# Attention preparation in 512-column instructions, a transposed attention output, and a list scheduler in the kernel

## The chip, the cores and the metric

The kernel runs on one core of a Trainium2 chip. The metric is the device time of one execution, in microseconds (us), shown as the median of some runs. A profile is one further execution taken by the hardware profiler. Engines are named as it names them: PE (TensorE matmul), PEld (its weight load), DVE (VectorE), ACT (ScalarE), POOL (GpSimd), and SP (SyncE), which here only issues DMAs. An engine takes its instructions strictly in the order in which they were issued to it.

## The reference

Gated linear attention over 4 batches, 8 heads, 768 tokens and head size 48, followed by an MLP with a rational activation on the 3072 tokens of width 8 x 48 = 384:

```python
for t in range(S):
    state = alpha[:, :, t, :, None] * state + np.einsum('bhd,bhe->bhde', k[:, :, t], v[:, :, t])
    y[:, :, t] = np.einsum('bhd,bhde->bhe', q[:, :, t], state)
...
x = np.ascontiguousarray(attn_out.transpose(0, 2, 1, 3)).reshape(B * S, H * D)
...
h = x @ w_in
h2 = h * h
h3 = h2 * h
P = a[0] + a[1] * h + a[2] * h2 + a[3] * h3
Q = 1.0 + np.abs(b[0]) * np.abs(h) + np.abs(b[1]) * h2
g = P / (Q + 1e-06)
return (g @ w_out).astype(np.float32)
```

q, k, v and alpha are float32; `w_in` (384 x 2048) and `w_out` (2048 x 384) arrive as float64.

## The kernel before

The tokens are cut into 12 blocks of 256 (`m`), each of two chunks of 128 (`cc`). The recurrence is replaced by chunked products: in a chunk, running products of alpha scale q and k, the masked score matrix gives the part of y from within the chunk, and a state of 48 x 48 per head carries the rest. Heads go in four pairs `p`, one head on partitions 0 to 47 and one on 64 to 111.

**Preparation.** For a pair and block, `load_pair` (L278) brings alpha, k and q in, with four DMAs each, in pieces of 32 tokens, so that the 32 x 32 transposes of DVE (`turn_a`, `turn_k`, `turn_q`, L299 to L305, 256 columns) put the head's dimension on partitions. Two scans per chunk follow, `suffix` (L308) and `prefix` (L328), of 128 columns each, with `least` (L314) and `inverse` (L321) between them, and POOL multiplies the result into k and q (L335, L339). The first two blocks come in token by token (L352) and are transposed by PE (`turn_nat`, L363).

**A piece** is a pair in a chunk; there are 96. `sc_mm` transposes k (L390, 112 columns) and forms the scores of the two heads (L394), each head into a PSUM bank of its own. `sc_evac` copies both to SBUF with two ACT instructions (L402, L403), `sc_mask` applies the causal mask on POOL (L407), `decay` scales the state on POOL (L414). `attn_mm` then adds to y, tokens on partitions: one matmul with the state (L426), two with the scores as weights (L434), and two that form k'v for the next state (L442), which `kv_add` adds on DVE (L456, one instruction per head; L454 for the first chunk of a batch). The scores of the next piece use the same two banks and wait for this one's copies and `kv_add`.

**From y to x.** After four pieces, `y_evac` (L460) copies y, PE transposes it (L465, three matmuls), and ACT and DVE split the result in two float32r parts (L469, L473), which are the MLP's moving operand x. There are three pairs of x buffers.

**The MLP** runs in 96 units `u`: a block times one of eight groups of 256 columns of `w_in`. `mlp_in` is 18 matmuls of 256 columns (L502), then ACT, POOL and DVE compute the activation on 512 columns (L510 to L562), and `mlp_out` is 12 matmuls of 384 columns (L572 with `gh`, L582 with `gl`). Three PSUM banks hold the h of three units. The first two blocks go through weight groups 0 to 3 first and 4 to 7 afterwards (`PHASES = (0, 4)`). The weights are converted from float64 words at the start by ACT, DVE and POOL, one group of `w_in` and one of `w_out` at a time (L218 to L247).

**Order.** All steps are added to a `Plan`; the order in which they are issued was worked out beforehand and is stored in the file as a packed list (`ORDER`). Semaphores follow from the tiles that instructions share.

Beside the work, 18 DMAs read alpha once more and ACT finds out whether every value lies in the range for which the chunked products hold (L612, L616); a general path, not taken here, follows otherwise.

Of the kernel before, what the change touches and what calls it, by code (L numbers as in the profile page):

```python
# [3 lines left out]

# [18 lines left out]
class Plan:  # L23
    """Steps with an engine, a rough length and what they wait for (after, and tiles taken and
    freed).  run() calls them in the order of ORDER, after a check that each comes behind
    what it waits for."""

    def __init__(self, bufs, last):
        self.steps = {}
        self.bufs = bufs  # L30

    def add(self, key, eng, cost, fn, args, after=(), takes=(), frees=(), due=None, lat=0.2):
        self.steps[key] = (fn, args, after)

    def run(self):
        keys = list(self.steps)
        order = np.frombuffer(zlib.decompress(base64.b85decode("".join(ORDER))), np.uint16)
        assert sorted(order) == list(range(len(keys)))
        done = set()
        for n in order:  # L40
            key = keys[n]
            fn, args, after = self.steps[key]
            assert all(a in done or a not in self.steps for a in after)
            fn(*args)
            done.add(key)


TB, GB, FB = 2, 4, 2
LAG, LAG_END, PACE, T0, SLACK, EARLY = 3.0, 2.0, 5.0, 30.0, 1.3, 8
GU0, GSTEP = 40, 1.5  # L50
NAT = 2
NB0 = 2
XH, ND = 4, 4
PHASES = (0, 4)
WB = 3
HB, U0, HY = 1, 0, 0
SB, YB, XB = 3, 2, 3


# the order of the plan's steps (each by its place among the plan's add calls)  # L60
ORDER = [
    'c-jTQ0{|E{5CFhWKKbO6R9kJXwr$(CZDX~z+ICmlwr$(CvAd4Y5B`BgFctQ|N$3ilp%e6gzo8p+fc`KIro&?R7rM',
    'YG02lzHVFnC@!7vEMKm(i!|G_v|0!yJ6%!aYh6B^=jXoP*BDGq@-umS|kh4HW+8skt{3Cmy@G(!myp*hZi2{0U*;',
    '6&&P2;H$atb&oS8aBc_m=7&*EsTIkuo)J@WS9c2uq7(!4t=pbw#Egp0oFhVj0<gW6GVc&&=K3>J~##YLBnY{0G;p',
    '*w8O~I1^esI&>5q^78rqDu@`p3gK!9X<5}o|=O7jQ0r8*@UW0zv6aR$k5Fh&EV;F>g;|+KMBnIG6OaKFM7~X{QFc',
    '@#caC{24fZ!W!gOT_QUchs>0|{Y(UI&vfH4MQ|phZ;p2Mw?osDHvsNCev<f=C1Z;$Zy?#^7NXq(|Wpy$kNb5g3gZ',
    'V5mL{X(2I;#b|I5g17`0(!nd(4G~3pxCh4|2}Ba(aF`yC|KV@Q0GEN`1iXd`2;wU2fH!a-qJx8pI0JLQWPAW`!9!',
    'Ar0RfW1PWS>-FakV+_i#u51u@|(%)^|p5|6`F6yhCRfmm=?XM}0^9b&_Dj4YDFOuVn-fE4d^Qt<=s=|?&R%t9q{!',
    '2>-TAHr6MBHruVFb6ZiT#P0j>xcTIo{xFpgH8#<^#aTcPjoRDp}**bI8tYUMfg-N#^mCYM)6e}u>|wNGyPdF#pik',
    '%T2UO5i1nBimSYLX1~2pqtOEJqn_h(_;k!;HQj1ccC_BUuKXhqu!i%k_DUJB4ql(>FL{x=8#cKSe{}3;ATCoOW3Z',  # L70
    'hrK8bqgLVlAc<)#0~}LF>>E&_CKzT(JSOiW<Nai{gll7*E6`N1Lz_q!6$5W{fX9#iloU3&y2D+b|Br7U{)bA_BeD',
    '@hFQpj)HQC_*4cGh=?TVU;P0RP(m?EM<S%r`XFW(+p#eu7LjQOj?p_Yk4Q+VC<^Vu{7@58ia#hdC8FFSG3~)xkcO',
    'H-bdiMeP;rr#nnGSGEYeX@$}9F_GbjrMpd4iorA2-!B{I-HOi$&hAneCtA|o}21NbM!5}BwF9l}H+GZlhtBBO{(`',
    'RFi4qXLwLZr~AY0fnI)6cx$nC}yR<r~;LTV^{=|Q#QJcwV@zYq7zs~6sGLdfO3hVP*&s<Md&0}fQFQUDvOj<QWT|',
    'ASP{-*4$4WVu^3f?T+|Zsi!+#;ic=k^OeMrQtVkuOGL#cdL`mvGIYkv}L|tjDK95!D5q^YHR2RnSYIFh1ivprLH4',
    '>$%9#j+;alEb|YS2||OqZ|>P0&rKpco`-(iOah)kITj1-0lFHlx}!lsb#M*i=*!-RL^DhB`EiZew%mLG_`kxQ{L9',
    '4i*wOu?@7Od)S>?QCX@Y9$*9LMGx@__N3M{oE~Fus!Jm&lV~W~P$yB3`p`erLJStQ#8hfaEk#Z76kCb5FhI1UzBG',
    '*{>e`})=px!d9np^_>H0K+>WcR8H?^n9x}KO$14Re=mu6B&>QB$Gffz;0XaIE;twm?*CI-?JJ(`wNFVRMfq3U85J',
    ';zQoOf(iNXe<q)8T0}h!eAOlv*{&f7OQ9oji*;wU(BHkVGm89*LXAZ6m7*^nn)c)5Ag<@i+R*c?4|bNEzTD!X+FK',
    'f)wGX#iv=`^*3bc(Oyk8unnG)75uKwUVjV4}?&5M7A<ok{F<h*tK4PeNkH2xG*g*f$e)@p_h$VE8Hqr%}D-O{|yh',  # L80
    'NL5v{*`qsh!wN4``40gh!~a*h2q`&)82KrBUJ`O%z}77_Ac*=__uf%XFL`(Koz8PiPyRpb28C-cDEPBz>aqc#U?^',
    'DOxXf&@_FWe&7NzU5^nr=rcX08Tu!#6{qPYeW71?hMv*Y@RV*5sBbh+JSVSi(^(oTv=S<cdO^WV5_f2dm?~b<WN}',
    '(Z^@{q72<9ujCRBGRqWM94g;MwEJ4H5ch}1OklipGc72oU=M$HlL=oc*()5U*chDcz3(-N^zL@|*J7^^ypgl4G_=',
    '036d!|bH@bTK$3&EMh!B{qMWpwP?|QOz=u!6>sqL{QPpB9YNt3eimxlgLC=G0aDbq>`FUMw`egnOP&U7&6O6O!Jr',
    'dLuEDlMRH@zpK6tusZ*FFs*s6gZiU+-rHO53>B1(JnXPXJXJ(10YK}fDGMg&KnrJGUDPpRc=qk0zZgz{=;#w$XVy',
    'aEzPKc+rh%{!S$YJ7`Sn80-X%2|Erno6;a+!GMMu@F)o0TH1$z$TEY9^g2VdAR1CcP<XYM6W`zB(*QnImGeXl4?q',
    '^s2PkDvpYj>X@i*YMO+qjA?FanMCS(NUUm`{APu?63UvSs*brI%9#S@t*C2~se-1wsb~IDEldSd-}Era)owa2TA2',
    'nWg}NnrnwI9EXl=HMk*1+(WA24U=22*CQmJ0Xo9&{aX=l!e9pa=&tty%JW|x?&E1M3cw@ITqnm%Tp{>OAOY1Mq)&',
    '!khGO=Hv7EYSa&CgyK*H)K#<On>t<%rzO+8!^C~6Q@K$HQMYHmqaEt(9APgRc1BFj55DP7IjxNHDk=<FxGT655hQ',
    ';O}!TL&0y2bj5pcUMbX_1G3UhulS2(P3(Yz+(d1N@MQ%08EHLX$E_FqeRg=xba8oQYdDLR_B)kp>%ztKzDXw0Gyl',  # L90
    'RO#XjY4<=AO7JHkb$Eniyu5nt1Yr*ktmlWu~$kZt|;#V!1hFMwkNXm$)D{npa}8nPyg)=i!4Wq~42XVx@T`wwOC&',
    'x>=}yidCktI$~y+t!9yaCuW)(qKJ|*u3W4ynZxEkT~vJ($INB3%@k9g#8GqH%r+&|cJnN(HapA-v&NKE-@{H*UtK',
    'XEOR4MPq}gTGn$qf&d17{(GU~CoW=@;Da*ugxUWPN~iMVdcsb}V?NGI=$v*w#AudW&)&lxQ%s8>PB&*FypZX(Ev>',
    'ZW;aDyhBZi})^Hm{+EXdM<96v~r($X{xFp=C!G&Zksn@zqw;-s`RpnI&Z40yXK9lp)Qzv=545@BFeAgt@$Q`y>Dt',
# [52 lines left out]
def tile_gla_then_rational_mlp(ctx, tc, q, k, v, alpha, w_in, w_out, ca, cb, out):  # L147
# [777 lines left out]
```

## Time and profile before

| what | value |
|---|---|
| median of 3 runs | 696.76 us (692.65 to 697.98) |
| span of the profiled execution, first to last instruction | 695.3 us |
| mean granted TensorE clock of that execution | 0.924 of full speed |
| DMA, whole span | 41.81 MB in 179975 packets, 169408 of them under 512 B |
| `w_in` and `w_out` | 16 DMAs of 768.0 KB |

A row of the profile by line reads: line, engine, operation, tile written and tiles read, shape, count, then total busy time in us and the mean of one instruction in ns, then the idle time of the engine just before those instructions and what ended it. A row of the timeline gives start and length in us, and an x with the number of instructions that were put together. A row by stage gives, for a stretch, the busy time of each engine with the number of its instructions. The chain of waits follows the work that ended last back to the start. Matmuls overlap, so the distance between their starts tells more than their length.

### The profile page before, as it was taken

How to read it: one execution, taken by the hardware profiler on the slowest of the kernel's cores; microseconds unless marked ns; L12 is line 12 of the kernel's file. 1: busy time of each engine (PE TensorE's matmuls, PEld its weight loads, DVE VectorE, ACT ScalarE, POOL GpSimd, SP SyncE). 2: the span in 40 equal slices, each digit the busy share in tenths (PEclk: the TensorE clock that was granted, in tenths of full speed). 3: DMA queues.
4: the chain of work that ended last, by engine and by line, in shares of the span. 5: the costliest groups of instructions: out<-in, count | busy, mean ns of one | idle time of the engine just before them, and what ended most of it. 6: DMA issues, size and time to landing. Idle time of an engine off the chain costs nothing.

```text
span 695.3 us, 12692 instructions
## 1 busy us (share of the span) xinstructions
PE 636.1 (91%) x4330; PEld 581.7 (84%) x4330; DVE 615.0 (88%) x1174; ACT 490.6 (71%) x947; POOL 414.0 (60%) x534
## 2 busy tenths in 40 slices
PE   5976799888999899989999999989998999999986
PEld 4765698677888899888888999978997899999985
DVE  5899989999999889998999899698999988976674
ACT  1345656766777798967877878776867787888683
POOL 2266758665565566744666666664746557756552
PEclk8557559899999999989999999999999999999999
DMA  9997541142422324444222231300422002000010
GB/s 188 216 236 162 122 106 24 19 71 39 63 41 54 71 49 76 76 94 88 37 29 55 30 57 25 58 1 8 78 43 52 2 1 58 1 2 1 1 46 27
DMA packets 179975, 41.81 MB, mean 60 GB/s; under 512 B 169408, under 2 KB 172480, under 8 KB 179904
## 3 DMA queue, kind: packets, MB, share of 16 engines
q1 hardware_dynamic: 179904, 40.94, 30.2%
q8 instruction: 36, 0.59, 0.3%
q14 instruction: 35, 0.29, 0.1%
HBM read 36.18 MB, written 4.72 MB: 59 GB/s over the span
## 4 chain that ended last, share of the span: by engine, by line
PE 47%; DVE 33%; issue 5%; ACT 5%; SPq 3%; DMA 3%; POOL 2%; DVEq 0%; ACTq 0%; POOLq 0%
PE ps_h L502 16%; PE ps_o L572 12%; PE ps_o L582 6%; DVE g L308 5%; PE ps_sc L394 4%; PE ps_y L434 4%; DVE t L543 4%; DVE ps_h L546 3%; DVE f L328 3%; DVE t L551 3%; SPq L278 3%; DVE t L531 3%; DVE t L534 3%; PE ps_sc L442 2%; PE ps_y L426 1%
## 5 line engine op out<-in xcount | busy, mean ns | idle before, releaser
L502 PE MATMUL ps_h<-x_hi,wi 128*128 128x256 f32 x1152 | 243.4, 298 | 16.7 <-DVE t L551 16.4
L502 PEld LDWEIGHTS ps_h<-x_hi,wi 128*128 128x128 f32 x1152 | 192.0, 195 | 28.7 <-DVE t L551 19.9
L562 POOL TENSOR_TENSOR gl<-t,gh 128x512 fp32r<-128x512 f32 x96 | 125.4, 1306 | 96.8 <-ACT gh L557 92.8
L572 PE MATMUL ps_o<-wo,gh 128*128 128x384 f32 x768 | 169.0, 356 | 0.0
L502 PE MATMUL ps_h<-x_lo,wi 128*128 128x256 f32 x576 | 166.1, 288 | 0.0
L572 PEld LDWEIGHTS ps_o<-wo,gh 128*128 128x128 f32 x768 | 136.6, 195 | 5.2 <-ACT gh L557 0.3
L521 POOL TENSOR_TENSOR qm<-qm,ah 128x512 f32<-128x512 f32 x96 | 126.9, 1323 | 20.1 <-ACT qm L518 16.3
L502 PEld LDWEIGHTS ps_h<-x_lo,wi 128*128 128x128 f32 x576 | 112.8, 196 | 0.1
L407 POOL TENSOR_SCALAR_AFFINE_SELECT sc<-sc 128x256 f32<-128x256 f32 x96 | 42.3, 442 | 114.2 <-ACT sc L403 107.7
L537 ACT ACTIVATE ps_h<-qm,one_eps 128x512 f32<-128x512 f32 x96 | 66.4, 692 | 46.6 <-DVE t L534 43.6
L582 PE MATMUL ps_o<-wo,gl 128*128 128x384 f32 x384 | 88.2, 352 | 0.0
L518 ACT ACTIVATE qm<-ah,bab 128x512 f32<-128x512 f32 x96 | 78.1, 813 | 10.5 <-DVE ps_h L546 9.7
L531 DVE TENSOR_TENSOR t<-t,ps_h 128x512 f32<-128x512 f32 x96 | 64.9, 676 | 21.9 <-ACT t L514 20.5
L543 DVE SCALAR_TENSOR_TENSOR t<-t,coef,ps_h 128x512 f32<-128x512 f32 x96 | 71.0, 740 | 9.0 <-ACT ps_h L540 7.6
L557 ACT ACTIVATE gh<-t 128x512 fp32r<-128x512 f32 x96 | 60.5, 631 | 23.8 <-DVE t L551 20.9
L514 ACT ACTIVATE t<-ps_h,coef 128x512 f32<-128x512 f32 x96 | 74.4, 775 | 4.1 <-PE ps_h L502 2.8
L394 PE MATMUL ps_sc<-tq,tk 48*128 48x128 f32 x384 | 62.1, 351 | 15.1 <-DVE st_s L456 13.5
L534 DVE SCALAR_TENSOR_TENSOR t<-t,coef,ps_h 128x512 f32<-128x512 f32 x96 | 71.0, 739 | 2.0
L434 PE MATMUL ps_y<-v,sc 128*128 128x48 f32 x384 | 62.3, 290 | 8.8 <-POOL sc L407 5.5
L582 PEld LDWEIGHTS ps_o<-wo,gl 128*128 128x128 f32 x384 | 68.8, 194 | 1.9 <-issue 0.2
L402 ACT ACTIVATE sc<-ps_sc 128x240 f32<-128x240 f32 (+1 forms) x96 | 33.9, 353 | 49.6 <-PE ps_sc L394 48.7
L394 PEld LDWEIGHTS ps_sc<-tq,tk 48*128 48x128 f32 x384 | 38.4, 204 | 36.2 <-DVE st_s L456 16.1
(79 smaller groups left out, 1075.3 us busy)
## 6 DMA issues: line engine op xcount, KB each, us to landing
wi_words<-in_moe_w_in_dram SPq DMA_DIRECT2D x8, 768.0 KB, 5.2
wo_words<-in_moe_w_out_dram SPq DMA_DIRECT2D x8, 768.0 KB, 5.5
v<-in_v_dram SPq DMA_DIRECT2D x24, 192.0 KB, 3.1
gt<-in_alpha_dram SPq DMA_DIRECT2D x18, 256.0 KB, 3.0
out_dram<-part SPq DMA_DIRECT2D x24, 192.0 KB, 2.0
raw_a<-in_alpha_dram SPq DMA_DIRECT2D x80, 32.0 KB, 2.2
raw_k<-in_k_dram SPq DMA_DIRECT2D x80, 32.0 KB, 2.2
raw_q<-in_q_dram SPq DMA_DIRECT2D x80, 32.0 KB, 2.2
```

The costliest lines, as they stand in the source:

```text
L394: nc.tensor.matmul(ms[i][j][:, c0 : c0 + C], kt_[r, cs], qt[r, cs], start=True, stop=True)
L434: nc.tensor.matmul(y[:, h, :], sc[:, j * C : (j + 1) * C], vt[:, h, :], start=(first and p == 0 and j == 0), stop=(p == NPAIR - 1 and j == 1),
L502: nc.tensor.matmul(hs[u][:, ff * SEG : (ff + 1) * SEG], split_w["i", j][:, kt * FU + ff, w, :], x[:, kt, :], start=(kt == 0 and n == 0), s ...
L514: nc.scalar.activation(t1s[u], hs[u], AF.Identity, bias=a2, scale=a3)
L518: nc.scalar.activation(qms[u], ahs[u], AF.Identity, bias=b0, scale=b1)
L521: nc.gpsimd.tensor_tensor(qms[u], qms[u], ahs.pop(u), op=ALU.mult)
L531: nc.vector.tensor_tensor(t1s[u], t1s[u], hs[u], op=ALU.mult)
L534: nc.vector.scalar_tensor_tensor(t1s[u], t1s[u], a1, hs[u], op0=ALU.add, op1=ALU.mult)
L543: nc.vector.scalar_tensor_tensor(t1s[u], t1s[u], a0, hs[u], op0=ALU.add, op1=ALU.mult)
L562: nc.gpsimd.tensor_tensor(gls[u].rearrange("p a b -> p (a b)"), t1s.pop(u), gh, op=ALU.subtract)
L572: nc.tensor.matmul(oacc[m][tt], ghs[u][:, ff, tt * P : (tt + 1) * P], split_w["o", j][:, ff, w, :], start=(j == j0 and ff == 0 and w == 0) ...
L582: nc.tensor.matmul(oacc[m][tt], gls[u][:, ff, tt * P : (tt + 1) * P], split_w["o", j][:, ff, 0, :], start=False, stop=(j == j1 and ff == F ...
```

## The change

The diff keeps the algorithm of the attention and of the MLP, and rewrites how the first is prepared, laid out and ordered.

* **Preparation.** Two pairs (`n`) with both chunks, four runs of 128 tokens, are prepared at once: transposes of 512 columns, one scan of 516 columns in each direction. A pad column of zeros in alpha cuts the product between the runs, and ones (or the inverses) added at the pad start the next. POOL's multiplies cover 512 columns. The way by token rows for the first two blocks is gone. A load call is 8 DMAs.
* **k is transposed inside the score matmul.** `tq` carries 64 columns of the identity behind the 128 of q, so a score matmul of 192 columns gives the scores and k's transpose. One ACT instruction copies both heads.
* **y is formed transposed.** v and the state are the weights, scores and q the moving operand; the two heads write partitions 0 to 63 and 64 to 127 of one bank. `x_hi` and `x_lo` read that bank; `y_evac` and the transposes of x are gone. Pair 3 holds the rows that fill the 16 unused partitions of the other three pairs; `x_gap` moves them with six SBUF-to-SBUF DMAs a block, and `load_w` brings `w_in` in the same arrangement of rows, with four DMAs in place of one.
* **State.** `kv_add` takes both heads in one instruction, and the decay of the state is inside it; `decay` on POOL makes the form that the matmul reads.
* **Buffers.** Two x buffers (three before), three `gh` and two `gl` (four and four), two work buffers for weights (three). PSUM is one tile with fixed banks. `PHASES = (0, 6)`.
* **Order.** `Plan.order` is a list scheduler that runs when the kernel is built: it models each engine with lengths from a table, a lock between some DVE steps and POOL, and one DMA stream, and takes the ready step with the earliest latest start. `PACE, T0, LEAD = 5.5, 32.0, 2.0` set the times at which steps are due.

The MLP's own instructions (L502 to L594) are as before.

```diff
-        nc.vector.transpose(ta[m, p], raw["a"][:, p, :])
+    def turn_a(n):
+        o = ta[n % 2][:, 1:].rearrange("p (c t) -> p c t", t=C1)[:, :, 0:C]
+        nc.vector.transpose(o, raw["a"][n % 2].rearrange("p a (c t) -> p (a c) t", t=C))
...
         nc.vector.tensor_tensor_scan(
-            tg[m, p][:, cc, 0:C][:, ::-1], al[:, ::-1], zeros, 1.0, op0=ALU.mult, op1=ALU.add
+            tg[n % NQ][:, ::-1], ta[n % 2][:, 1:][:, ::-1], ones1, 0.0, op0=ALU.mult, op1=ALU.add
...
+    def inverse(n):
+        t = d1[n % 2][:, 0 : NC4 * C1 : C1]
+        nc.vector.tensor_scalar(t, tg[n % NQ][:, 0 : NC4 * C1 : C1], 2.0 ** -60, None, op0=ALU.max)
         nc.vector.reciprocal(t, t)
...
+            fp[n % 2], ta[n % 2][:, 0 : NC4 * C1], d1[n % 2], 0.0, op0=ALU.mult, op1=ALU.add
...
-        if not last:
-            nc.tensor.transpose(ms[i][0][:, 0:ROWS], kt_[0:ROWS, cs], ident[0:ROWS, 0:ROWS])
+        w = C if last else C + DP
         for j in range(2):
-            r = slice(64 * j, 64 * j + D)
-            c0 = (ROWS, 0)[j]
+            r = slice(DP * j, DP * j + D)
+            o = b0_ + (S0, BANK)[j]
             nc.tensor.matmul(
-                ms[i][j][:, c0 : c0 + C], kt_[r, cs], qt[r, cs], start=True, stop=True
+                ps[:, o : o + w], tk[n % NQ][r, c, :], tq[n % NQ][r, c, 0:w], start=True, stop=True
             )
...
-        nc.scalar.activation(scs[i][:, c0 : ROWS + C], ms[i][0][:, c0 : ROWS + C], AF.Copy)
-        nc.scalar.activation(scs[i][:, ROWS + C :], ms[i][1][:, 0:C], AF.Copy)
+        nc.scalar.activation(scs[i % 3][:, :, 0:w], src[:, :, 0:w], AF.Copy)
...
+        for j in range(2):
+            r = slice(DP * j, DP * (j + 1))
+            yr = y[r, p * C : (p + 1) * C]
+            if not first:
+                nc.tensor.matmul(
+                    yr, st_d[p][:, j, :], tq[n % NQ][:, c, 0:C], start=(p == 0), stop=False,
+                    skip_group_check=True,
+                )
+        for j in range(2):
+            r = slice(DP * j, DP * (j + 1))
+            yr = y[r, p * C : (p + 1) * C]
             nc.tensor.matmul(
+                yr, vt[:, p + NPAIR * j, :], sc[:, j, 0:C], start=(first and p == 0),
+                stop=(p == NPAIR - 1), skip_group_check=True,
             )
...
+            nc.vector.scalar_tensor_tensor(
+                st_s[p], st_s[p], tg[n % NQ][:, C1 * c : C1 * c + 1], kv, op0=ALU.mult, op1=ALU.add
+            )
...
+    def x_gap(m):
+        x = xts[m % XB].bitcast(F32)
+        for j in range(2):
+            for kt in range(KT):
+                nc.sync.dma_start(
+                    x[DP * j + D : DP * (j + 1), :, kt, :],
+                    x[DP * j + GAP * kt : DP * j + GAP * (kt + 1), :, KT, :],
                 )
...
+        for nm in "akq":
+            add(("ld", nm, n), "SP", 0.5, load_akq, (nm, n), [("t" + nm, n - 2), ("set", nm, n % 2)], kb=1.9)
...
+        add(("xh", g), "ACT", 0.6, x_hi, (g,), [("am", NPAIR * g + NPAIR - 1), ("last", m - XB)])
+        add(("xl", g), "DVE", 0.7, x_lo, (g,), [("xh", g)])
+        if cc:
+            add(("xg", m), "SP", 0.4, x_gap, (m,), [("xl", g), ("xl", g - 1)], kb=0.6)
```

More of the change, by code (lines that the diff above doesn't have):

```diff
@@ L710, in tile_gla_then_rational_mlp @@
     NUA = len(jobs)
[L711 to L713 removed]
+    plan = Plan()
     add = plan.add
[L717 to L724 removed]
```

958 lines of the change are left out of this document (439 added, 519 removed).

## The prediction

> **What bounds the kernel now.** I read the page first, then a table of busy time by stage, then the chain of waits, then the PE timeline of one stretch, and last the groups by line and shape.
>
> ```profile
> span 695.3 us, 12692 instructions
> ...
> PE 636.1 (91%) x4330; PEld 581.7 (84%) x4330; DVE 615.0 (88%) x1174; ACT 490.6 (71%) x947; POOL 414.0 (60%) x534
> ...
> PE 47%; DVE 33%; issue 5%; ACT 5%; SPq 3%; DMA 3%; POOL 2%; DVEq 0%; ACTq 0%; POOLq 0%
> ```
>
> Two engines carry the chain. A mean over the run hides where, so the next view cuts the span at two points: 213 us, where the sixteenth of the 96 MLP units is through, and 634 us, where the attention is over. The last two rows count L502 (18 matmuls a unit) and L394 (4 records a piece) in the middle stage.
>
> ```profile
> 0.00:213.00 213.00, 178.12 (x1047) 155.69 (x1047) 197.38 (x402) 122.52 (x231) 125.35 (x171) 0.79 0.50 105
> 213.00:634.00 421.00, 405.35 (x2935) 374.71 (x2935) 380.36 (x717) 326.75 (x650) 260.49 (x341) 0.98 0.24 43
> 634.00:695.00 61.00, 52.62 (x352) 51.34 (x350) 37.22 (x57) 41.36 (x68) 28.18 (x23) 0.98 0.06 21
> ...
> 213.00:634.00 421.00, 168.03 (x1224) 152.29 (x1224) 0.98 0.24 43
> ...
> 213.00:634.00 421.00, 36.24 (x256) 22.21 (x256) 0.98 0.24 43
> ```
>
> Columns are PE, PEld, DVE, ACT, POOL busy, then granted clock, DMA share and GB/s. Stage 1 is DVE's (197 of 213 us, few matmuls). Stage 2 is shared, PE 405 and DVE 380 of 421. It holds 1224/18 = 68 units and 256/4 = 64 pieces. Matmul records overlap, so I price PE by the distance between starts:
>
> ```profile
> 559.81 2.14 PE ps_h L502 x18
> ...
> 561.79 0.26 PE L390 MATMUL ps_sc<-ident,tk 112*128 112x112 f32 x1
> 561.98 0.49 PE L394 MATMUL ps_sc<-tq,tk 48*128 48x128 f32 x4
> 562.40 0.55 PE L465 MATMUL ps_x<-ident,ys 128*128 128x128 f32 x3
> 562.71 0.37 PE L502 MATMUL ps_h<-x_hi,wi 128*128 128x256 f32 x1
> ...
> 564.92 0.87 PE L572 MATMUL ps_o<-wo,gh 128*128 128x384 f32 x4
> 565.63 0.86 PE L582 MATMUL ps_o<-wo,gl 128*128 128x384 f32 x4
> 566.33 1.57 PE L572 MATMUL ps_o<-wo,gh 128*128 128x384 f32 x8
> 567.74 0.36 PE L426 MATMUL ps_y<-st_d,tq 112*128 112x96 f32 x2
> 567.93 0.57 PE L434 MATMUL ps_y<-v,sc 128*128 128x48 f32 x4
> 568.43 0.29 PE L442 MATMUL ps_sc<-v,sc 128*48 128x48 f32 x4
> 568.66 0.97 PE L582 MATMUL ps_o<-wo,gl 128*128 128x384 f32 x4
> ```
>
> An MLP unit is 2.14 us of `mlp_in` and 12 x 2.82/16 = 2.12 of `mlp_out`, 4.26 together. A piece is 0.61 (transpose and scores, 561.79 to 562.40), 0.92 (`attn_mm`, 567.74 to 568.66) and a quarter of 0.31 (three transposes of x): 1.61. Stage 2 holds 68 x 4.26 + 64 x 1.61 = 393 us of PE work in 421, 93%. It is close to PE-bound, with DVE right behind.
>
> **The change, part by part.**
>
> *PE, scores.* The 112-column transpose of k goes; the two score matmuls stream 192 columns in place of 128. These rows are of two windows that end just after the first L394 record:
>
> ```profile
> 404.52 0.37 PE L394 MATMUL ps_sc<-tq,tk 48*128 48x128 f32 x1
> ...
> 404.52 0.38 PE L394 MATMUL ps_sc<-tq,tk 48*128 48x128 f32 x2
> ```
>
> The records of the two heads start within 0.01 us of each other, yet four take 0.42 (561.98 to 562.40), 0.21 a pair. That is about two weight loads: L434, which moves only 48 columns per 128-column load, still takes 0.50/4 = 0.125 each. So I read the pair as bound by its loads, with the streaming side by side. Then 192 columns fit under the loads: 0.42, plus 0.09 for the change of shape (L390 took 0.19 for 112 columns where one of the three 128-column transposes takes 0.10), 0.51. If streams follow one another, a pass costs 0.105 x 192/128 = 0.158, four 0.63, with the change-over 0.72.
>
> *PE, output.* State and y become 2 + 2 matmuls of 128 moving columns against 64-column weights, one per half of the array's columns. Side by side: four passes of 0.107, 0.43, plus 0.23 for the kv matmuls (568.43 to 568.66) and 0.09, 0.75. In sequence: 0.86 + 0.23 + 0.09 = 1.18. The transposes of x (0.08 a piece) go in both cases. A piece thus costs 1.26 or 1.90 against 1.61. I take 1.26, since the two-record row shows starts together. Stage 2 then needs 290 + 64 x 1.26 = 371 us of PE; the other end is 412.
>
> The Trainium skill, "TensorEngine Tiling (Array Packing)", section Tiling Modes under Key Properties, says that different tiles can execute both weight loads and matmuls in parallel. Read in full, a score pair would cost one 192-column pass (0.158) and a piece 0.41 + 0.75 = 1.16, which takes 64 x 0.10 = 6 us off the sum. The rows speak for parallel streams (equal starts) and against parallel loads (0.21 for a pair of 128 columns, where the full rule gives about 0.11), so I keep my price; the 6 us lie inside my own range.
>
> *DVE.* Two chunks of two pairs are prepared by one instruction each.
>
> ```profile
> L328 DVE TENSOR_TENSOR_SCAN f<-ta,rb,zeros 128x128 f32<-128x128 f32 x80 | 65.0, 825 | 0.6
> L531 DVE TENSOR_TENSOR t<-t,ps_h 128x512 f32<-128x512 f32 x96 | 64.9, 676 | 21.9 <-ACT t L514 20.5 <-PE ps_h L502 0.8
> L308 DVE TENSOR_TENSOR_SCAN g<-ta,zeros 128x128 f32<-128x128 f32 x80 | 61.9, 790 | 0.4
> L456 DVE TENSOR_TENSOR st_s<-ps_sc,st_d 48x48 f32<-48x48 f32 x128 | 25.5, 199 | 17.0 <-PE ps_sc L442 14.7 <-ACT gh L557 0.7 <-POOL st_d L414 0.4
> L314 DVE TENSOR_SCALAR rb<-g 128x2 f32<-128x2 f32 (+1 forms) x56 | 22.4, 405 | 0.5
> L299 DVE STREAM_TRANSPOSE ta<-raw_a 128x256 f32<-128x256 f32 x40 | 17.0, 427 | 0.2
> L473 DVE TENSOR_TENSOR x_lo<-ps_x,x_hi 128x384 fp32r<-128x384 f32 x24 | 13.0, 544 | 4.9 <-ACT x_hi L469 4.9
> L328 DVE TENSOR_TENSOR_SCAN f<-ps_t,rb,zeros 128x128 f32<-128x128 f32 x16 | 7.4, 470 | 0.1
> L308 DVE TENSOR_TENSOR_SCAN g<-ps_t,zeros 128x128 f32<-128x128 f32 x16 | 6.3, 411 | 7.9 <-PE ps_t L363 7.8
> ...
> 0.00:213.00 213.00, 25.66 (x40) 0.79 0.50 105
> ```
>
> The same 128-column scan takes 411 and 470 ns with its data in PSUM and 790 and 825 with it in SBUF: 0.37 us on the average is a wait, not work. L531 against L473 gives (676 - 544)/128 = 1.03 ns a column and 0.15 us fixed, so a scan runs at (411 - 150)/128 = 2.04 ns a column, and 516 columns cost 1.20 us. With one wait of 0.37 each, 48 scans cost 75 us against 140.6 now: -65. `least` goes from 56 to 24 at 0.4: -13. Transposes: 120 of 0.43 become 72 of 0.69, about 0. State sums: L456 and its copies, 160 at 0.2, become 80: -16. `x_lo` grows from 384 to 512 columns, 24 x 0.13 = +3. Together -91 us. If the longer instructions meet longer waits (double, 0.74), 18 less; if a scan's fixed part is all of its excess over 1.03 ns a column, 48 x 0.4 = 19 more. The last row counts L308 in stage 1, 40 of 96; by that share the -91 are -38 there and -53 in stage 2, whose DVE falls to 327 of 421.
>
> *ACT and POOL.*
>
> ```profile
> L339 POOL TENSOR_TENSOR tq<-tq,f 128x256 f32<-128x256 f32 x40 | 30.9, 774 | 7.6 <-DVE f L328 3.6 <-DVE rb L314 2.2 <-DVE tq L305 1.8
> L335 POOL TENSOR_TENSOR tk<-tk,g 128x256 f32<-128x256 f32 x40 | 27.2, 682 | 6.1 <-DVE g L308 3.2 <-DVE tk L302 2.9
> L402 ACT ACTIVATE sc<-ps_sc 128x240 f32<-128x240 f32 (+1 forms) x96 | 33.9, 353 | 49.6 <-PE ps_sc L394 48.7
> L403 ACT ACTIVATE sc<-ps_sc 128x128 f32<-128x128 f32 x96 | 26.5, 276 | 8.5 <-PE ps_sc L394 8.5
> ```
>
> Two score copies become one of 384 columns: (353 - 276)/112 = 0.69 ns a column, 0.45 us, 96 x (0.63 - 0.45) = -17 on ACT, and the copy of y goes. POOL's multiplies, 80 in 58 us, become 48 of twice the length, at most 48 x 1.5 = 72: +14. Neither engine is on the path (ACT 327 and POOL 260 of 421), so I cost both at 0; the cover is PE's 371.
>
> *SP and x.* The 16 gap rows of x are filled by six DMAs a block, which wait for `x_lo`; behind them on SP stand the next loads of alpha, k and q, and DVE's transposes wait for those. `mlp_in` of a new block waits for their landing.
>
> ```profile
> 404.83 4.82 SPq L278 DMA_DIRECT2D raw_k<-in_k_dram  x8
> ...
> raw_a<-in_alpha_dram SPq DMA_DIRECT2D x80, 32.0 KB, 2.2
> ...
> PE ps_h L502 <- DVE t L551: 4.9, 9, 1.3
> PE ps_sc L394 <- DVE st_s L456: 4.9, 6, 2.2
> ```
>
> An issue is 4.82/8 = 0.60 us, so six are 3.6 and land 2.2 later: 5.8 us. I cost them at 0: only two x buffers are left in place of three, but `x_hi` of block m needs only the last `mlp_in` of block m-2, which is 8 units, about 8 x 5.5 = 44 us, ahead of its own use. The weights of `w_in` come in 32 issues in place of 8, 24 x 0.60 = 14 us more on SP in stage 1, also at 0: DVE's 197 us cover it, and the DMA engines are busy 0.50 of the stage. The score and the y banks are as many as before; `gh` and `gl` have three and two buffers in place of four, so PE has to take an output within two units, which I cost at 0 as long as PE runs in step; if it lags, `pool_gl` stops POOL.
>
> *Order.* The list scheduler's order is not in any trace. I bound it by the share of PE work in stage 2: 93% as now, up to 99%. The last two rows (waits of PE in stage 2) are DVE's doing, 9.8 us; with a lighter DVE I halve them and take 95%.
>
> *Sum.* Stage 1: DVE's -38, less 12 that I give back because the first block's loads are now 48 issues x 0.60 = 29 us on SP, ahead of which DVE has little to do: -26, ends -38 and 0. Stage 2: 371/0.95 = 390, -31; ends 371/0.99 = 375 (-46) and 412/0.93 = 443 (+22). Stage 3 has no attention and keeps its 61. Together 695.3 - 57 = 638; the median of the runs, 696.76, lies 1.5 above the profiled span, so 640.
>
> **The rivals.**
>
> *Streams in sequence.* The score and output matmuls of the two heads do not overlap. For it: a pair at exactly twice 0.105. Stage 2 takes 412/0.95 = 434, +13; with stage 1's -26 the time is 684.
>
> *Stage 1 keeps its length.* The early loads on SP and not DVE set it; for it: DMA share 0.50 and 105 GB/s there, against it DVE's 197 of 213. 640 + 26 = 666.
>
> *x comes late (slower).* SP takes its queue in order. If three calls of eight loads (3 x 4.82 = 14.5 us) stand ahead of the gap DMAs, x is 14.5 + 5.8 = 20 us late after `x_lo`. A block's second chunk needs four pieces one after another, and the lead of 44 us would be used up at about 6 us apiece. Eleven blocks that each stop PE by more than (57 + 7)/11 = 5.8 us make it slower than before by 1%; at 7 us it is 640 + 77 = 717. Against it: 0.60 us an issue is 72 x 8 x 0.60 = 346 us of SP in a span of 640.
>
> **How the numbers follow.** A measurement of this kernel can tell about 1% from no change. Chances: the forecast 0.62 (640; its own range 613 to 660, from the best ends of both stages, 695.3 - 38 - 46 + 1.5, to stage 2 at 93%, 371/0.93 = 399, with half of stage 1's gain), stage 1 unshortened 0.10 (666), streams in sequence 0.14 (684, a third of it within 1%), x late 0.14 (704 and up, a little of it within 1%). Faster: 0.62 + 0.10 + 0.09 = 0.81; within 1%: 0.06; slower 0.13. The range leaves out 0.04 below and the slower case above: 605 to 694.
>
> **What would show it.** The start of the first output matmul to the first kv matmul near 0.43 us confirms the side-by-side reading, 0.86 refutes it. Scans of 516 columns near 1.2 us without a wait, 1.6 on the average, and DVE near 524 us in all confirm DVE's part. The stages should last 187, 390 and 61 us. Waits of L502's successor on a gap DMA, of microseconds a block, would make the forecast wrong, and so would a sixteenth unit that is through only at 213 us.

## The result: 31 us slower, and where they went

The changed kernel takes 727.9 us (median of 4 runs, 724.8 to 729.0) against 696.4 for the kernel before (692.7 to 698.0): a ratio of 1.045, interval 1.042 to 1.049. The forecast was 640, the range 605 to 694. The page of the changed kernel (span, busy time, chain by engine, start of the chain by line):

```profile
span 725.9 us, 12443 instructions
...
PE 592.8 (82%) x4290; PEld 521.0 (72%) x4290; DVE 534.1 (74%) x806; ACT 479.1 (66%) x827; POOL 443.8 (61%) x518
...
PE 49%; DVE 13%; SPq 12%; DMA 10%; ACT 9%; issue 4%; POOL 1%; DVEq 0%; ACTq 0%; POOLq 0%
```

PE has 43 us less work than before (636.1) and DVE 81 less (615.0), as the change meant, and the span is 31 us longer. DVE's part of the chain falls from 33% to 13%, and SP's queue and the DMAs, 6% before, hold 22% of it. A table of busy time (PE, PEld, DVE, ACT, POOL) shows where:

```profile
0.00:213.00 213.00, 113.28 (x695) 94.77 (x696) 135.02 (x181) 87.83 (x138) 116.29 (x159) 0.87 0.53 96
0.00:252.00 252.00, 145.03 (x917) 122.41 (x918) 162.62 (x223) 112.88 (x182) 139.64 (x183) 0.88 0.50 91
```

In its first 213 us DVE was busy for 197; now for 135, and PE has done 113 us of work where it had done 178. No engine is busy for even two thirds of that time; all of them wait. The sixteenth unit is through at 252 us, 39 later. The next two rows count L398 (4 records a piece) and L503 (18 a unit) behind that point:

```profile
252.00:726.00 474.00, 42.28 (x276) 21.97 (x274) 0.98 0.24 45
```

```profile
252.00:726.00 474.00, 189.09 (x1386) 174.96 (x1386) 0.98 0.24 45
```

The same 77 units, and 276/4 = 69 pieces where 64 were left before, take 474 us against 482. So the 31 us are +39 in the start and -8 behind it; the prediction had -26 and -31.

**The start.** SP's queue, in order of time:

```profile
0.81 0.40 SPq L214 DMA_DIRECT2D wi_words<-in_moe_w_in_dram  x1
...
2.68 5.30 SPq L324 DMA_DIRECT2D raw_a<-in_alpha_dram  x8
...
9.94 5.49 SPq L324 DMA_DIRECT2D raw_a<-in_alpha_dram  x8
15.47 4.03 SPq L324 DMA_DIRECT2D raw_k<-in_k_dram  x8
19.55 3.90 SPq L324 DMA_DIRECT2D raw_q<-in_q_dram  x8
23.49 3.90 SPq L324 DMA_DIRECT2D raw_k<-in_k_dram  x8
27.44 3.90 SPq L324 DMA_DIRECT2D raw_q<-in_q_dram  x8
31.38 1.08 SPq L333 DMA_DIRECT2D tv<-in_v_dram  x2
32.58 4.16 SPq L324 DMA_DIRECT2D raw_a<-in_alpha_dram  x8
36.78 0.45 SPq L223 DMA_DIRECT2D wo_words<-in_moe_w_out_dram  x1
37.36 4.13 SPq L324 DMA_DIRECT2D raw_k<-in_k_dram  x8
41.59 3.89 SPq L324 DMA_DIRECT2D raw_q<-in_q_dram  x8
45.52 0.45 SPq L214 DMA_DIRECT2D wi_words<-in_moe_w_in_dram  x1
```

In these 46 us SP goes from one step to the next almost without a pause. A load call of eight DMAs holds it 3.9 to 5.5 us (3.9/8 = 0.49 an issue, gaps included), while the scheduler's table gives the call 0.5 us. The calls of 5 us and more have stops inside them (last section). The first six calls are the first block's; those from 32.58 on are for the second, and the first tile of `w_out` (36.78) stands behind the first of these, the third tile of `w_in` (45.52) behind three. The kernel before brings its first two blocks in with 24 DMAs (L352), the changed kernel with 96: that is 72 issues more, some 35 us of SP at 0.49 each. The chain of the first 230 us carries it:

```profile
by line: SPq L324 22.4%; DMA wi_words<-in_moe_w_in_dram 11.7%; DMA wo_words<-in_moe_w_out_dram 9.4%; PE ps L503 6.1%; issue 5.9%; DMA x<-x 4.4%; PE ps L564 3.3%; DVE wr L245 2.2%; PE ps L398 2.1%; DVE fp L356 1.9%; SPq L214 1.8%; DVE wo_wor
```

### The profile page after: what moved, and what is told of

It reads as the page before. It is cut to its first block, busy times and chain, and to the rows that moved or that the text cites. A ratio compares the mean times of both kernels' runs of the same rounds, so it can differ in the third digit from the quotient of the medians.

```text
span 725.9 us, 12443 instructions
## 1 busy us (share of the span) xinstructions
PE 592.8 (82%) x4290; PEld 521.0 (72%) x4290; DVE 534.1 (74%) x806; ACT 479.1 (66%) x827; POOL 443.8 (61%) x518
## 4 chain that ended last, share of the span: by engine, by line
PE 49%; DVE 13%; SPq 12%; DMA 10%; ACT 9%; issue 4%; POOL 1%; DVEq 0%; ACTq 0%; POOLq 0%
PE ps L503 19%; PE ps L564 14%; SPq L324 9%; PE ps L574 7%; PE ps L398 4%; DMA wi_words<-in_moe_w_in_dram 4%; DMA wo_words<-in_moe_w_out_dram 3%; PE ps L430 3%; ACT ps L530 2%; PE ps L437 2%; DVE t L537 2%; ACT ps L533 2%; DVE t L527 2%; DVE ps L540 2%; DVE t L523 2%
## 5 line engine op out<-in xcount | busy, mean ns | idle before, releaser
L503 PE MATMUL ps<-x,wi 128*128 128x256 f32 x1728 | 244.1, 293 | 29.7 <-DMA x<-x 18.0
L503 PEld LDWEIGHTS ps<-x,wi 128*128 128x128 f32 x1728 | 227.2, 198 | 39.9 <-issue 14.5
L564 PE MATMUL ps<-wo,gh 128*128 128x384 f32 x768 | 165.6, 359 | 27.6 <-ACT gh L549 26.6
L564 PEld LDWEIGHTS ps<-wo,gh 128*128 128x128 f32 x768 | 135.0, 196 | 43.8 <-ACT gh L549 30.7
L537 DVE SCALAR_TENSOR_TENSOR t<-t,coef,ps 128x512 f32<-128x512 f32 x96 | 70.9, 739 | 85.3 <-ACT ps L533 85.2
L398 PE MATMUL ps<-tq,tk 48*128 48x192 f32 (+1 forms) x384 | 69.0, 394 | 54.5 <-POOL tq L374 37.0
L574 PE MATMUL ps<-wo,gl 128*128 128x384 f32 x384 | 89.9, 358 | 0.3 <-POOL gl L553 0.3
L398 PEld LDWEIGHTS ps<-tq,tk 48*128 48x128 f32 x384 | 37.0, 202 | 72.7 <-POOL tq L374 37.7
L523 DVE TENSOR_TENSOR t<-t,ps 128x512 f32<-128x512 f32 x96 | 65.3, 680 | 26.0 <-ACT t L513 25.8
L513 ACT ACTIVATE t<-ps,coef 128x512 f32<-128x512 f32 x96 | 73.7, 768 | 1.2 <-POOL gl L553 1.2
L527 DVE SCALAR_TENSOR_TENSOR t<-t,coef,ps 128x512 f32<-128x512 f32 x96 | 71.7, 747 | 2.8
L574 PEld LDWEIGHTS ps<-wo,gl 128*128 128x128 f32 x384 | 68.4, 197 | 4.5 <-issue 2.5
L546 DVE SCALAR_TENSOR_TENSOR t<-ps,t 128x512 f32<-128x512 f32 x96 | 66.3, 691 | 3.1
L540 DVE SCALAR_TENSOR_TENSOR ps<-qm,ps 128x512 f32<-128x512 f32 x96 | 66.1, 688 | 0.0
```

The source lines that it names most:

```text
L398: nc.tensor.matmul(ps[:, o : o + w], tk[n % NQ][r, c, :], tq[n % NQ][r, c, 0:w], start=True, stop=True)
L503: nc.tensor.matmul(h_of(u)[:, ff * SEG : (ff + 1) * SEG], split_w["i", j][:, kt * FU + ff, w, :], x[:, xp, kt, :], start=(kt == 0 and n == ...
L523: nc.vector.tensor_tensor(t, t, h_of(u), op=ALU.mult)
L527: nc.vector.scalar_tensor_tensor(t, t, a1, h_of(u), op0=ALU.add, op1=ALU.mult)
L537: nc.vector.scalar_tensor_tensor(t, t, a0, h_of(u), op0=ALU.add, op1=ALU.mult)
L540: nc.vector.scalar_tensor_tensor(h_of(u), buf(s, "qm", u), 1.0 + 1e-6, h_of(u), op0=ALU.add, op1=ALU.mult)
```

## The experiments on the start

The table gives, for each kernel, when the last step of DVE in the first and in the seventeenth unit starts (L546 in the changed kernel, L551 before, L544 in e8; the second of these points is the one called "sixteenth unit through"), the rest of the span behind that, and the median of the runs, all in us.

| kernel | first unit | 16th through | rest | time | ratio to before (interval) |
|---|---|---|---|---|---|
| before | 76 | 213 | 482 | 696 | |
| changed | 94 | 252 | 474 | 728 | 1.045 (1.042 to 1.049) |
| e1_issue_lengths | 85 | 230 | 465 | 694 | 0.998 (0.996 to 1.001) |
| e2_two_queues | 83 | 240 | 472 | 714 | 1.027 (1.023 to 1.031) |
| e3_phases04 | 98 | 265 | 475 | 742 | 1.066 (1.063 to 1.069) |
| e5_table_queues | 94 | 227 | 464 | 692 | 0.996 (0.994 to 0.997) |
| e6_weights4 | 76 | 213 | 468 | 683 | 0.983 (0.980 to 0.986) |
| e8_no_gap | 88 | 244 | 466 | 712 | 1.026 (1.021 to 1.032) |
| e11_tb3 | 70 | 208 | 468 | 677 | 0.974 (0.970 to 0.978) |

**SP's lengths in the table.** The third number of `add` is the length of the step; `kb` is the time that the scheduler gives its transfer on the DMA stream. The two lines shown stand for seven: the four DMAs of `w_in` go from 0.3 to 1.85, single DMAs from 0.07 or 0.1 to 0.4 or more.

```diff
-            add(("ld", nm, n), "SP", 0.5, load_akq, (nm, n), [("t" + nm, n - 2), ("set", nm, n % 2)], kb=1.9)
+            add(("ld", nm, n), "SP", 3.9, load_akq, (nm, n), [("t" + nm, n - 2), ("set", nm, n % 2)], kb=0.2)
...
-            add(("xg", m), "SP", 0.4, x_gap, (m,), [("xl", g), ("xl", g - 1)], kb=0.6)
+            add(("xg", m), "SP", 3.8, x_gap, (m,), [("xl", g), ("xl", g - 1)], kb=0.6)
```

> The changed kernel, with one thing altered: the list scheduler's table gets the lengths that SP's DMA issues show in its trace (a load of alpha, k or q 3.9 us in place of 0.5, a w_in half 1.85 in place of 0.3, the gap of x 3.8 in place of 0.4, single DMAs 0.4 to 0.9 in place of 0.07 to 0.1). No instruction is added or taken away, only the order differs. Theory (the start is bound by SP's issues, which the order made for an SP eight times as fast has the wrong way round): the first unit is through near 80 us in place of 94, the sixteenth near 225 in place of 252, the time 700 (690 to 712). Rival, the DMA engines or the weights' transfers bound the start, whatever stands first on SP: 721 to 735. Rival, the order as such is a gamble: it can come out on either side by more than 10 us without the first unit moving.

694 us: the whole loss is gone with no instruction changed. The 16th unit comes 22 us earlier; the first gains 9, not the 14 expected. The edit also shortens the transfer of a load call in the model (`kb` 1.9 to 0.2), so the gain belongs to SP's entries as a whole and not to one number.

**Half of the early loads from another queue.**

```diff
-                nc.sync.dma_start(
+                (nc.scalar if n < 4 and g >= 2 else nc.sync).dma_start(
```

> The changed kernel in its own order, but of each of the first twelve load calls four of the eight DMAs are issued from ACT's queue: 48 issues of about 0.45 us, 22 us, leave SP. Theory (SP's issues bind the start): everything that stands behind them on SP comes up to 22 us earlier, the first unit at about 80 us in place of 94, the sixteenth near 235 in place of 252, the time 705 to 718. Rival, the DMA engines' throughput or the weights' transfers bind it: first and sixteenth unit move by less than 5 us, 722 to 735 (ACT issues 22 us more, which could add a little).

714 us, the 16th unit at 240: 12 of the 22 us of issues taken off SP come out at that point, in the old order. Issues are on the path, not only the order.

**Fewer weights ahead of the second block.**

```diff
-PHASES = (0, 6)
+PHASES = (0, 4)
```

> The changed kernel with the first two blocks taken through columns 0 to 3 of the MLP first, in place of 0 to 5, so that the first eight units need four pairs of weight tiles and not six for twelve units; the order is made anew with the table as it is. Theory (SP's issue of the loads binds): the first twelve units still wait for the same things, 720 to 735. Rival, the change of this size made the start late, since more weights are wanted before the second block: 700 to 715, with the sixteenth unit near 235.

742 us, slower than both theories have it. The rival (fewer weights, earlier start) falls; that a new order from the wrong table can cost another 14 us was not expected, and why this one does was not followed up.

**Both, and then the weights' length.** e5 splits the early loads, on the base of e1, as planned steps of SP and ACT; e6 changes in e5 the transfer times alone, and `kb=0.2` of half a load call to 0.5.

```diff
+            if n < 4:
+                add(("ld", nm, n), "SP", 1.95, load_akq, (nm, n, (0, 1)), ld_old, kb=0.2)
+                add(("ld2", nm, n), "ACT", 1.95 + 0.1, load_akq, (nm, n, (2, 3), nc.scalar), ld_old, kb=0.2)
...
-        add(("w", key), "SP", 1.85 if key[0] == "i" else 0.45, load_w, key, kb=2.0)
+        add(("w", key), "SP", 1.85 if key[0] == "i" else 0.45, load_w, key, kb=4.0)
```

> The kernel of e1_issue_lengths (the table with SP's measured lengths), and in it the first twelve load calls are split: four DMAs on SP, four on ACT's queue, each half a step of its own of 1.95 us in the table. Theory (SP's issues still bind the start: L324 issues are 27% of its chain and 36% of the first 130 us): 22 us of issues leave SP, the first unit is through near 70 us in place of 85, the sixteenth near 215 in place of 230, the time 680 (672 to 688), faster than the kernel before. Rival, with the order put right the DMA engines bind the start (busy 0.84 between 60 and 100 us): within 4 us of 694.

> As e5_table_queues, and the table also gives the transfer of a weight tile 4.0 us in place of 2.0 (768 KB at the 190 GB/s of the busiest stretch) and that of half a load call 0.5 in place of 0.2. Only the order differs from e5. Theory (issues bind, transfers do not): within 6 us of e5. Rival (weight transfers that are taken for half their length still put the order wrong): a further gain of 8 us or more, the sixteenth unit before 210.

e5: 692, within the rival's 4 us of 694; with SP's lengths right in the table, taking issues off SP is worth 2 us, hardly more than the noise, where it was worth 14 in the old order. Its first unit is even 9 us later than in e1, where 15 us earlier were expected. e6: 683, 9 us better, so the theory falls there too: the transfers, of the weights above all, taken for half their length, still put the order wrong. Of the 45 us between the changed kernel and e6, 34 came with SP's lengths, 2 with the second queue, 9 with the weights'. But the 16th unit is now where it was before, at 213, neither below 210 as the rival has it nor at 187 as predicted. Busy time in e6 up to there:

```profile
0.00:213.00 213.00, 145.15 (x926) 123.63 (x926) 163.09 (x228) 111.18 (x177) 140.81 (x185) 0.89 0.58 103
```

DVE has lost 34 of its 197 us, near the 38 predicted, and the stage is as long as before. So DVE's work did not set its length.

**Without the gap DMAs.**

```diff
-        for j in range(2):
-            for kt in range(KT):
-                nc.sync.dma_start(
-                    x[DP * j + D : DP * (j + 1), :, kt, :],
-                    x[DP * j + GAP * kt : DP * j + GAP * (kt + 1), :, KT, :],
-                )
```

> The changed kernel in its own order without the six DMAs a block that fill the gap rows of x: these rows stay zero (set once at the start), so the output misses head 7's part of the MLP's input. Theory: the gap costs its place in the queue and its landing, about 7 us, at the first two or three blocks, where PE waits for x (18 us in three waits), and nothing later: 708 to 718. Rival of the prediction's sum (the gap is hidden): 723 to 730. Rival (each block stops PE for it): 12 blocks by 5 us, 670 or less.

712 us: the gap costs 16, as the theory has it in sum, though not in place: 8 us of it lie behind the 16th unit, where I expected none.

## The experiments behind the start

**PE's price of a piece**, from the PE timeline of the changed kernel:

```profile
470.41 0.44 PE L430 MATMUL ps<-tq,st_d 128*64 128x128 f32 x4
470.68 0.39 PE L437 MATMUL ps<-sc,tv 128*64 128x128 f32 x4
470.90 0.27 PE L445 MATMUL ps<-tv,sc 128*64 128x48 f32 x4
471.10 1.31 PE L503 MATMUL ps<-x,wi 128*128 128x256 f32 x9
472.35 0.60 PE L398 MATMUL ps<-tq,tk 48*128 48x192 f32 x4
472.87 1.66 PE L564 MATMUL ps<-wo,gh 128*128 128x384 f32 x8
```

`attn_mm` takes 0.69 from start to start (470.41 to 471.10) and the scores 0.52 (472.35 to 472.87): the heads do run side by side. Over the whole trace the medians are 0.69 and 0.53. To these comes an entry: the start after an L503 comes 0.117 us later (median) if it is another L503, 0.206 if it is an L398; after an L564 0.174, or 0.268 if it is an L430. That is 0.09 twice a piece, 1.39 in all against 1.26 predicted and 1.61 before. From the first output matmul to the first kv matmul (470.41 to 470.90) it is 0.49, near the 0.43 that was to confirm the side-by-side reading and far from 0.86. By that price the rest holds 77 x 4.26 + 69 x 1.39 = 424 us of PE work in 474, 89%; before it was 77 x 4.26 + 64 x 1.61 = 431 in 482, also 89%.

**What holds the 89%.** Three kernels in the order of the changed kernel, so that only work differs: e7 leaves out 6 of the 18 matmuls of `mlp_in`, e13 the scans and the step between them (`suffix`, `inverse`, `prefix`) from the seventh preparation on, e14 both.

```diff
-            for n, (w, xp) in enumerate(((0, 0), (0, 1), (1, 0))):
+            for n, (w, xp) in enumerate(((0, 0), (1, 0))):
...
     def suffix(n):
+        if n >= 6: return
```

> The changed kernel in its own order, but the product of x's low part with w_in is left out of mlp_in (12 matmuls a unit in place of 18), so the output misses that small term. PE loses 6 x 0.117 = 0.70 us a unit, nothing else changes. Theory (after the start PE's work sets the pace): from the sixteenth unit to the last the kernel gains some 0.8 of 79 x 0.70 = 55 us, the time is 675 to 692. Rival (the round trip of a unit through ACT, DVE and POOL or DVE's work sets the pace): less than 20 us, 708 to 728.

> The changed kernel in its own order, but from the seventh preparation on the two scans and the step between them (L346, L352, L353, L356) are left out and old factors are used, so the output is not the reference's. DVE loses 18 x (1.44 + 0.65 + 1.53) = 65 us, all of it after the first 150 us; PE has all its work. Theory (after the start the ring of DVE and ACT with DVE's preparation between is on the path as much as PE): 20 to 40 us less, 688 to 708. Rival (PE's 5.65 us of work a unit and piece hold it, against a pace of 5.8): 10 us less at most, 718 to 728.

> e13_no_scans and e7_no_xlo in one: the scans are left out and x's low part too, in the order of the changed kernel. PE loses 67 us and DVE 65. Theory (the two hold the pace side by side, so that taking either away leaves the other): clearly more than the two gains together, 50 us or more below the changed kernel, 678 or less. Rival (one of the two alone holds it): about the sum of the two gains. Rival (a ring of hand-overs of 4.9 to 5.1 us a unit, to which the attention adds little): no more than 45 us, since 79 units at 5.2 take 411 us of the 462 that they take now.

Measured: 717.8, 720.8 and 695.3 us, that is -10, -7 and -33; behind the 16th unit alone -7, -4 and -25. In e7 and e13 the rival holds. Neither PE's 67 us nor DVE's 65 do much alone, and together they do twice the sum of the two. Busy time from 350 to 450 us in e7, e13 and e14:

```profile
350.00:450.00 100.00, 95.35 (x670) 82.08 (x669) 85.54 (x135) 82.22 (x149) 70.71 (x80) 0.96 0.32 56
```

```profile
350.00:450.00 100.00, 100.00 (x771) 89.52 (x769) 72.61 (x121) 82.99 (x148) 66.52 (x79) 0.98 0.33 58
```

```profile
350.00:450.00 100.00, 99.02 (x736) 85.84 (x735) 77.49 (x128) 88.34 (x158) 72.45 (x86) 1.00 0.31 52
```

With the scans gone (second row) PE shows no idle time and the units follow each other at 5.8 us for long stretches; I take that for PE's bound, 0.15 above the 5.65 that I count for a unit and a piece. With PE relieved (first row) the units beside a preparation keep the 5.7 and 6.3 us that they take in the changed kernel, and the others fall from 5.7 or 5.8 to about 5.3. (The granted clock is 0.96 there and 0.98 in the changed kernel; that takes back 2% of PE's time, some 9 us in 474, too little to hide a gain of 55.) With both gone the pace is 5.1 to 5.3 and falls no lower: the rival with the ring was the nearer one (45 us at most), and my 50 us or more was too much. The ring is to be seen behind the attention, where the pace is 4.9 to 5.3 us in the changed kernel too:

```profile
694.42 0.68 DVE L523 TENSOR_TENSOR t<-t,ps 128x512 f32<-128x512 f32 x1
...
695.13 0.75 DVE L527 SCALAR_TENSOR_TENSOR t<-t,coef,ps 128x512 f32<-128x512 f32 x1
...
695.98 0.69 ACT L530 ACTIVATE ps<-qm,one_eps 128x512 f32<-128x512 f32 x1
...
696.70 0.58 ACT L533 ACTIVATE ps<-ps 128x512 f32<-128x512 f32 x1
...
697.32 0.75 DVE L537 SCALAR_TENSOR_TENSOR t<-t,coef,ps 128x512 f32<-128x512 f32 x1 [1.44 <-ACT ps L533]
...
697.98 0.69 DVE L540 SCALAR_TENSOR_TENSOR ps<-qm,ps 128x512 f32<-128x512 f32 x1
...
698.70 0.69 DVE L546 SCALAR_TENSOR_TENSOR t<-ps,t 128x512 f32<-128x512 f32 x1
699.31 0.68 DVE L523 TENSOR_TENSOR t<-t,ps 128x512 f32<-128x512 f32 x1
...
700.02 0.75 DVE L527 SCALAR_TENSOR_TENSOR t<-t,coef,ps 128x512 f32<-128x512 f32 x1
```

L527 to L527 is 4.89 us (695.13 to 700.02): five DVE steps, and two of ACT that overwrite the bank which L523 and L527 read. DVE stands still for 1.44 of them.

**The scans put back in four.** e4 has the four scans of 129 columns that one of 516 replaces, in the same order.

```diff
-            tg[n % NQ][:, ::-1], ta[n % 2][:, 1:][:, ::-1], ones1, 0.0, op0=ALU.mult, op1=ALU.add
+        for c in reversed(range(NC4)):
+            cs = slice(C1 * c, C1 * (c + 1))
+                tg[n % NQ][:, cs][:, ::-1], ta[n % 2][:, 1:][:, cs][:, ::-1], ones1[:, 0:C1], 0.0,
```

> The changed kernel in its own order, with each merged scan of 516 columns put back as four scans of 129 columns: 192 scans in place of 48. By the scans of the kernel before (790 and 825 ns each) DVE gets some 80 us more work. Theory (in the changed kernel DVE's saving lies off the path: DVE is idle for most of the first 150 us, and later PE sets the pace): the time grows by less than 10 us, 724 to 738. Rival, the merging does pay and only the start hides it: at least half of the 80 us shows, 765 or more.

745.5 us, +17.5, between the two. DVE's busy time rose by 25 us (558.7 against 534.1), not by 80, and 70% of that shows. One row of its groups says why it is not 80:

```profile
L361 DVE TENSOR_TENSOR_SCAN fp<-ta,d 128x129 f32<-128x129 f32 x96 | 49.9, 579 | 0.3
```

A scan of the old length takes 579 ns here and took 825 in the kernel before. So merging as such saved little more than a third of what the prediction put down to it; the rest came with the new arrangement. The traces show where these means come from. Scans from SBUF beside which POOL runs no instruction take 0.44 us in the kernel before (42 of 160) and 0.40 in e4 (92 of 192); the others take 0.94 and 0.77 on the average. So a smaller share of the scans meets POOL at work in the new arrangement. A scan of 516 columns without POOL takes 1.22 us (7 of 48), and short ones that follow each other in e4 start 0.30 to 0.33 us apart, so four are hardly more work than a long one. How POOL makes a scan wait, no run tests.

**Opening the ring.** From the twentieth unit on, L537, L540 and L546 of a unit are put behind L523 and L527 of the next (e9, e10 on the base of e6); e11 gives t a third buffer on the base of e6, e12 both.

```diff
+        for u in range(20, 95): steps["p", u]["after"].append(("t3", u + 1)), nxt["t3", u + 1].append(("p", u))
...
-TB = 2
+TB = 3
```

> The kernel of e6_weights4 (683 us), in which from the twentieth unit on the second half of a unit on DVE (L537, L540, L546) stands behind the first half of the next unit (L523, L527), in place of ahead of it; the order before that unit is the same. In e6 and in the changed kernel DVE's L537 of a unit waits for ACT's L533, that for L530, that for L527 of the same unit, and that stands behind L546 of the unit before: a ring of 3.56 us of DVE and 1.27 of ACT with its hand-overs, 4.9 us a unit, and 5.1 us is the pace of the units after the attention, though PE has only 4.2 us of work in them. Theory (this ring sets the pace where there is no attention, and holds PE back beside it): the last 20 units run at 4.3 to 4.6 us in place of 5.1, the time falls by 12 to 25 us, 658 to 671. Rival (PE's work or buffers set the pace and DVE's wait costs nothing): within 5 us of 683.

> The order of e9_loop, and as in e7_no_xlo the product of x's low part with w_in is left out (0.70 us of PE a unit less, the output misses that small term). Theory (with the ring opened, PE's work is what sets the pace): 30 us or more below e9_loop, where e7 gained 10 on the changed kernel. Rival (ACT or DVE's own work, 4.7 and 5.2 us a unit with the attention's share, sets it then): less than 15 us below e9_loop.

> The kernel of e6_weights4 with three buffers for t (L513 to L553) in place of two; the room comes from v, which has two in place of three; the order is made anew. In e9_loop the second half of a unit waited for the first half of the next, and that for the buffer of t that POOL's L553 gave back late, so both together made a ring of 7.6 us. Theory (the two buffers of t hold the pace): the scheduler uses the third by itself, the units after the attention run at 4.3 to 4.8 us in place of 5.1, 665 to 678. Rival (DVE's and ACT's order holds the pace, whatever the buffers): within 8 us of 683.

> e11_tb3 with the order of e9_loop from the twentieth unit on (second half of a unit behind the first half of the next on DVE). Theory (with a third buffer of t the ring of e9 is open and the ring of 4.9 us too): the units after the attention run at 4.3 to 4.8 us, 660 to 675. Rival (the reversed order makes a long ring whatever the buffers, by way of the three banks of h): 720 or more, as e9 did.

830.6, 825.9, 677.5 and 724.3 us. The reversed order does not open the ring, it makes a longer one. Two rows of the waits of e9:

```profile
DVE t L523 <- ACT t L513: 224.4, 70, 6.2
ACT t L513 <- POOL gl L553: 110.6, 69, 3.0
```

With two buffers of t, L513 of a unit waits for POOL to give back the buffer of the unit two before, and the first half of the next unit waits for L513: 7.6 us a unit. Since that ring holds e9, PE's relief in e10 is worth 5 us. A third buffer cuts it (e12 against e9) but not to below e6, so the reversed order is no gain in either form; e12's rival, 720 or more, holds. e11 without it is the fastest kernel of all, 2.6% below the kernel before, and inside both the theory's range and the rival's. But the units behind the attention still take 4.9, where 4.3 to 4.8 were expected, and its 16th unit is 5 us earlier than e6's with the rest the same. Its gain therefore came in the start, not by the mechanism that I gave: the theory's range was hit by luck. Whether it came by t's buffer, v's or the new order stays open.

## Why the prediction was wrong, step by step

- **Stage 1, -26: wrong, by 65 us; this is the failed step.** It took DVE's -38 for the stage's gain and gave back 12 for 29 us of issues "on SP, ahead of which DVE has little to do". It asked what bounds the stage now and not what does once DVE is lighter. The +39 are the order, made by a table that gives SP an eighth of its time: with SP's lengths mended 22 of them go (e1), with the second queue and the transfer times too all 39 (e6). The missing -26 are another matter. In e6 DVE has its 34 us less work and the stage is 213 us long, as before: the rival "stage 1 keeps its length" was the better half of the truth, and it had no bound on the side of a worse order. What holds e6's start is not isolated. SP's issues and the weights' transfers are the largest shares of the changed kernel's chain there, and the 29 us of issues that the prediction set down are for the first block alone, where the two blocks need some 35 us more than before. No run puts the old way of loading them back.
- **The order, bounded by PE's share in stage 2 only.** Behind the 16th unit, stages 2 and 3 together, the share came out as before (89%; the forecast's own figures make 91). The order's risk lay in stage 1, for which no bound was set. Both lengths were at hand: 0.5 for `load_akq` in the diff, 4.82 in a row that the prediction quotes.
- **`w_in` in 24 more issues, at 0.** The cover named was DVE's 197 us, and the change takes it away: DVE is busy 135 of 213. What these issues cost by themselves, no run shows.
- **The gap, at 0:** 16 us (e8).
- **x late, the rival with 5.8 us a block:** not what happened. PE waits for the gap DMAs three times in the whole run, all three before 252 us:

```profile
PE ps L503 <- DMA x<-x: 18.0, 3, 10.5
```

- **PE's piece, 1.26: right mechanism, mis-sized,** 1.39: the heads run side by side. The 0.09 for the change of shape was in the sum, once for the scores and once for the output, and it is what the trace shows. Of the 0.13 missing, 0.10 lie in the scores: the prediction let 192 columns fit under the loads, at 0.42, but the four matmuls take 0.53 (median of 73 calls), and 0.42 only where they stream 128 columns (16 calls), in the last chunk of a batch. By 64 x 0.13 that is 8 us. The Trainium skill, "TensorEngine Tiling (Array Packing)", Key Properties, says that changing the tiling mode drains TensorE; the 0.09 us at each entry agree with it. By the full parallel reading of that page, which the prediction weighed, a piece would cost 1.16; the 1.39 speak against it.
- **DVE, -91: -81.** The scans cost what was said, 71 us against 75, and by the split that was said: 1.22 us without a wait, against 1.20. This part of the sum held, and it did not set the time:

```profile
L356 DVE TENSOR_TENSOR_SCAN fp<-ta,d 128x516 f32<-128x516 f32 x24 | 36.8, 1535 | 0.3
...
L346 DVE TENSOR_TENSOR_SCAN tg<-ta,ones 128x516 f32<-128x516 f32 x24 | 34.6, 1442 | 0.2
```

- **ACT and POOL, at 0:** POOL's busy time grew by 30 us, not by 14. Behind the 16th unit PE waits 10.6 us for ACT's `gh` (five waits) and under 1 for POOL, so 0 was nearly right there.
- **Behind the 16th unit, -31: -8.** The 23 us are 8 for the piece, 7 for five more pieces that lie behind that point (5 x 1.39), and some 8 for a share that did not rise from 89 to 91 (the prediction's 451 us for 328 + 64 x 1.26 = 409 of work). The five pieces are not the late start's doing, since e6, which has no late start, has four more there (272/4 = 68). The share did not rise because PE and DVE hold the pace by turns (e7, e13, e14).

As a balance: 640 + 26 for a stage 1 of unchanged length + 17 for a rest of 468 instead of 451 is 683, which is what e6 takes. This only places the loss; it is no proof of a cause. The other 45 us, 39 in the start and 6 behind it, went with the mended table and, for 2 of them, with the second queue.

## What to carry to other kernels

Where an order is computed from a table, hold each length in it against a row of a trace before anything else is predicted: here SP's entries, eight DMA issues at the price of one above all, were worth 34 of 45 us, and the mended table, with half of the early loads on a second queue, turns a kernel 4.5% slower into one 1.7% faster. When an engine that bounds a stage is relieved, name what is late next in that stage and price it by its own queue, in order. And a bound that two engines hold by turns shows only when both are relieved: each alone was worth 10 us or less, both 33.

## What the runs showed of the hardware

Two queues that issue share one limit. In e6 ACT and SP both start at 0.81 us:

```profile
0.81 5.26 ACTq L324 DMA_DIRECT2D raw_a<-in_alpha_dram  x8
0.81 0.40 SPq L214 DMA_DIRECT2D wi_words<-in_moe_w_in_dram  x1
1.27 0.42 SPq L217 DMA_DIRECT2D wi_words<-in_moe_w_in_dram  x1
...
5.83 0.31 SPq L214 DMA_DIRECT2D wi_words<-in_moe_w_in_dram  x1
```

SP's third issue, which the program lets go at once and which in the changed kernel follows at 1.74 us, comes at 5.83. Counted from issue to landing, at most eight DMAs are under way at any time in all 16 traces, both queues together. In the changed kernel the eighth issue starts at 4.13 us and the next four at 4.83, 5.46, 6.90 and 7.67, each 0.02 us after one of the first four, the DMAs of a `w_in` tile, has landed. So a load call behind weight tiles holds SP for 5.3 us, and once for 10.0, in place of 3.9, and long transfers cost SP's time too. That the number eight itself is the limit is read from these counts; no run tests it.

The Trainium skill, "DMA: Bandwidth & Descriptors", Issuing engines are not separate DMA queues, says that a second issuing engine saves only the sequencer's issue time, and that this is usually small beside the DMA. The first half agrees with e2 (12 us for 22 of issues). The second does not fit the loads of 16 to 32 KB here: an issue takes 0.45 us against 2.0 from issue to landing, and eight in a row hold the queue for 3.9.
